# Two fp32 layers behind attention on one core: another order of the seven products, other banks, other homes

## The chip, the cores and the metric

The kernel runs on one core of one Trainium2 chip. The metric is the device time of one execution in microseconds; a kernel's time is the median of its runs. A core has TensorE (matmuls into the eight banks of PSUM), VectorE, ScalarE and GpSimd for element work, and SyncE, whose queue issues the DMAs here. Each engine works through its own instructions in a fixed order; a semaphore holds an instruction until what it needs is done, and everything behind it on that engine waits too.

## What is computed

Attention with a window of 128 over 4 x 8 heads of 576 positions, then two feed-forward layers on the 2304 x 512 tokens that come out, all in fp32:

```python
attn_out = _attn_ref(q, k, v)                      # window 128, slopes per head, softmax
x = attn_out.transpose(0, 2, 1, 3).reshape(2304, 512)
g = x @ w_gate; val = x @ w_val                    # layer one, 512 -> 1536
x = (g * sigmoid(g) * val) @ w_out                 # 1536 -> 512
h = x @ w_in                                       # layer two, 512 -> 2048
y = (h * tanh(softplus(h))) @ w_out                # 2048 -> 512
```

## The kernel before

**fp32 as three products.** TensorE multiplies in a rounded format (F32R). Every fp32 operand is split into a high part (rounded on ScalarE, `hi_act`, line 124) and a low part (the rest, on VectorE, `lo_dve`, line 127), and each product is three matmuls: high x high, high x low, low x high. All are issued at line 117. A tile that is split is therefore ready only when both engines have had it.

**Layer one** runs over five chunks of tokens (512, 384, 512, 512, 384). For each of 12 slices of the 1536 there is a pair of groups `g`, `v` (`gv_groups`: the hidden values into `g_ps`, then two VectorE steps at lines 603 and 611, then the split into `hh` and `hl`) and a group `o` that multiplies `hh`, `hl` by the output weights into four accumulators `acc0` to `acc3`. `o` runs some slices behind `g`, `v`: that distance is the lag, `CFG["lastlag"]` in the last chunk. At the end `evacuate` copies the accumulators out, two by ScalarE (line 580) and two by VectorE (line 581), as `ev`.

**Layer two** uses a scheme of the Winograd kind: a 2 x 2 block product with seven products rather than eight, of sums of blocks. It runs in three passes `p` over two blocks of TB = 384 tokens each.

- *First product* (`hidden`, for each of eight `j`): TensorE multiplies `win` (the weights' sums, split) by `xs1` to `xs7` (the tokens' sums, split) in the order 1, 6, 7, 5, 2, 4, 3, six matmuls each; product 2 adds onto the bank of 1, and 3 onto the bank of 5, so a `j` needs five banks. VectorE's `add` (line 666) and ScalarE join them to the hidden values `G`. The tokens' sums `xr` are made by VectorE (line 666).
- *The weights' sums* (`make_win`): four subtractions on GpSimd (line 754) into a tile `t4`, then the split into `win`, ScalarE and VectorE in two steps each, one from the raw weights `w4` and one from `t4`. There is one buffer for `t4`: GpSimd starts on the next when both engines have read it.
- *Second product*: for each product `i` of ORDER2, and each of four `q`, `operands` gives one split tile `op` of sums of `G` (five buffers), which TensorE multiplies by `wout` for m = 0 and m = 1, six matmuls each. So `i` takes 48 matmuls and two banks, a pass 336. `outputs` joins the products to `v` and `y` on VectorE (line 666), and ScalarE copies product 2 (line 860). Product 4 stays in its bank until 7 is done; then `done(2, ...)` subtracts it (`y<-v,bk`), which frees the bank.
- *Loads and stores*: `wout` comes in halves of 1 MB (line 763, three buffers), a pass 14 of them; a finished block of 768 tokens goes out as `yT` (line 865). Both stand in SyncE's queue.

**Banks.** `bank` (lines 654 to 659) hands out two kinds in turn: one of four that rotate, and one of four that are fixed by name, `acc0` to `acc3`, in a ring. A bank is written again when its last reader is done.

**Homes.** Tiles of layer two lie where layer one's tiles lay before them, on the weight tiles `wt` of the last chunk and others; each waits until the last reader of what it lies on is done. Which `wt` that is follows from the order in which the tiles of the pool `br` are asked for; `wt` of slice i is free when group i of the last chunk is done.

**Order.** TensorE's order is that of the program text. For the other engines a planner sets the order by its own idea of the times when the program is built; it is fixed then.

Of the kernel before, what the change touches and what calls it, by code (L numbers as in the profile page):

```python
# [29 lines left out]

SLOT = {1: 0, 2: 1, 3: 2, 5: 3, 6: 4, 7: 5, 4: 6}
CFG = dict(
    order="SSOTT", delay0=2, early=[4], pbufs=10, pump_g=2, pump_p=2, lag=4, lastlag=4, evprio=500,
    conv_a=0.1, conv_b=0.9,
)

# [60 lines left out]
def body(ctx: ExitStack, tc: tile.TileContext, qT, kT, vP, w1, w1o, w2, cst, yT):  # L97
# [495 lines left out]
    def gv_groups(ci, i):  # L593
        p = plansA[ci]
        n = p.n
        st = {}

        def g():
            need(("w", i))
            st["g"] = hid(x_t[ci], n, wt[i], 0)  # L600
            t = hp_.tile([128, 512], F32, tag="t", name="t")
            tanhs.append(nc.scalar.activation(out=t[:, :n], in_=st["g"][:, :n], func=AF.Tanh, scale=0.5))  # L602
            nc.vector.scalar_tensor_tensor(  # L603
                out=t[:, :n], in0=t[:, :n], scalar=1.0, in1=st["g"][:, :n], op0=ALU.add, op1=ALU.mult
            )
            st["t"] = t

        def v():
            vps = hid(x_t[ci], n, wt[i], 512)
            t = st["t"]  # L610
            nc.vector.scalar_tensor_tensor(  # L611
                out=t[:, :n], in0=t[:, :n], scalar=0.5, in1=vps[:, :n], op0=ALU.mult, op1=ALU.mult
            )
            if ci == len(plansA) - 1:
                hh = bpool["p"].tile([128, 512], F32R, tag="hhb", name="hh", bufs=CFG["lag"])
                hl = bpool["p"].tile([128, 512], F32R, tag="hlb", name="hl", bufs=CFG["lag"])
            else:
                hh = hp_.tile([128, 512], F32R, tag="hh", name="hh", bufs=2)
                hl = hp_.tile([128, 512], F32R, tag="hl", name="hl", bufs=2)
            hi_act(hh[:, :n], t[:, :n])  # L620
            lo_dve(hl[:, :n], t[:, :n], hh[:, :n])
            hs["A", ci, i] = (hh, hl)

        return [g, v]
# [29 lines left out]
    def bank():  # L654
        banks[0] += 1
        c, odd = divmod(banks[0], 2)
        if odd:
            return rot("bk")
        return ps.tile([128, 512], F32, tag=f"acc{c % CT}", name="bk", bufs=1)
# [24 lines left out]
            )  # L684
        return r

    def x_parts(bp, r):
        xs = {i: bp.tile([128, 2, 2, TB], F32R, tag=f"xs{i}", name=f"xs{i}", bufs=1) for i in range(1, 8)}
# [12 lines left out]
        part(xs[5], a22)  # L701
        part(xs[3], a12)
        return xs

    def products(bk, ws, xs, first, last):

# [4 lines left out]
            mm(o, wh, xl, False, False)  # L711
            mm(o, wl, xh, False, last and c == n - 1)

    def outputs(i, bk, u, new, done):


        bk = bk[:, :TB]
        if i == 1:
            u["c"] = new()
            nc.scalar.activation(out=u["c"], in_=bk, func=AF.Copy)  # L720
        elif i == 6:
            u["a"] = u.pop("c")
            add(u["a"], u["a"], bk)
        elif i == 7:
            u["b"] = new()
            add(u["b"], u["a"], bk)
        elif i == 5:
            done(3, u["b"], bk)
        elif i == 2:
            done(0, bk, None)  # L730
        elif i == 3:
            done(1, u["a"], bk)
        else:
            done(2, u["b"], bk)

    def layer2(br):
        G = {}
        win, wout = {}, {}
        ORDER1 = (1, 6, 7, 5, 2, 4, 3)
        ORDER2 = (4, 1, 6, 7, 5, 2, 3)  # L740
        onto = {2: 1, 3: 5}

        raws = {}

        def load_raw(p, j):
            raws[p, j] = br.tile([128, 4, 256], F32, tag="w4", name="w4", bufs=2)
            nc.sync.dma_start(out=raws[p, j], in_=w2d[j].rearrange("p (k n) -> p k n", k=4))

        def make_win(p, j):

            w = raws.pop((p, j))
            x = br.tile([128, 4, 256], F32, tag="t4", name="t4", bufs=1)
            for o, a, b in ((0, w[:, 0], w[:, 1]), (1, w[:, 3], x[:, 0]), (2, w[:, 3], w[:, 0]), (3, x[:, 1], w[:, 2])):
                nc.gpsimd.tensor_tensor(out=x[:, o], in0=a, in1=b, op=ALU.subtract)  # L754
            t = win[p, j] = br.tile([128, 2, 7, 256], F32R, tag="win", name="win")
            for d, src in ((slice(0, 3), w[:, 1:4]), (slice(3, 7), x)):
                hi_act(t[:, 0, d], src)
                lo_dve(t[:, 1, d], src, t[:, 0, d])
# [6 lines left out]
        def hidden(p, j, xs):  # L765
            w = win.pop((p, j))
            q, jj = divmod(j, 2)
            if jj == 0:
                G[p, q] = bp.tile([128, 4, 2, TB], F32, tag=f"g{q}", name="G", bufs=1)
            g = G[p, q]  # L770
            u = {}

            def new():
                return bp.tile([128, TB], F32, tag="u", name="u", bufs=6)

            def done(k, a, b):
                if b is None:
                    mish(g[:, k, jj], a)
                    return
                add(g[:, k, jj], a, b, ALU.subtract if k == 2 else ALU.add)  # L780
                mish(g[:, k, jj], g[:, k, jj])

            bks = {}
            for i in ORDER1:
                bk = bks[i] = bks[onto[i]] if i in onto else bank()
                s = SLOT[i]
                products(
                    bk, [(w[:, 0, s, c:c + 128], w[:, 1, s, c:c + 128]) for c in (0, 128)],
                    [(xs[i][:, 0, c], xs[i][:, 1, c]) for c in range(2)], i not in onto, i not in onto.values(),
                )  # L790
                outputs(i, bk, u, new, done)

        def operands(p, i):

# [12 lines left out]
                    add(g[:, 2], g[:, 1], g[:, 0], ALU.subtract)  # L807

        load_raw(0, 0)
        xr = load_x(br, 0)  # L810
        load_raw(0, 1)
        xs = x_parts(br, xr)
        for j in range(2):
            make_win(0, j)
            load_raw(0, j + 2)
# [2 lines left out]
        for p in range(NPB):  # L818
# [16 lines left out]
            left = [[2, 2], [2, 2]]  # L835
            t0 = 2 * p * TB
            for i in ORDER2:
                bks = held[i] = held[onto[i]] if i in onto else [bank(), bank()]
                for q, o in enumerate(operands(p, i)):
                    k, jq = divmod(2 * q, NJ // 2)  # L840
                    if (p, i, k) not in wout:
                        load_wout(p, i, k)
                        loads.remove((i, k))
                    w = wout[p, i, k]
                    if jq == 0 and loads:
                        load_wout(p, *loads.pop(0))
                    for m in range(2):
                        products(
                            bks[m],
                            [(w[:, jq + e, 0, 128 * m:128 * m + 128], w[:, jq + e, 1, 128 * m:128 * m + 128]) for e in range(2)],  # L850
                            [(o[:, 0, e], o[:, 1, e]) for e in range(2)],
                            i not in onto and q == 0, i not in onto.values() and q == NJ // 2 - 1,
                        )
                for m in range(2):

                    def done(k, a, b, m=m):
                        t, f = divmod(k, 2)
                        y = ys[f][m]
                        if b is None:
                            nc.scalar.activation(out=y[:, t], in_=a, func=AF.Copy)  # L860
                        else:
                            add(y[:, t], a, b, ALU.subtract if k == 2 else ALU.add)
                        left[f][m] -= 1
                        if not left[f][m]:
                            nc.sync.dma_start(out=yr[:, 2 * f + m, t0:t0 + 2 * TB], in_=y.rearrange("p a t -> p (a t)"))
# [7 lines left out]
                    outputs(i, bks[m], us[m], new, done)  # L873
                    if i == 7:
                        done(2, us[m]["b"], us[m]["p4"])
                if p + 1 < NPB:
                    if i == 7:
                        xs = x_parts(br, xr)
                    if i in (5, 2):
                        j = (5, 2).index(i)  # L880
                        make_win(p + 1, j)
                        load_raw(p + 1, j + 2)

# [164 lines left out]
```

## Time and profile before

| what | us |
|---|---|
| median of 3 runs | 1038.94 |
| lowest and highest of them | 1038.35, 1039.30 |
| profiled execution, its own time | 1040.23 |
| span of its profile | 1038.4 |

The profiled execution is 1.29 us above the median. TensorE is the busiest engine; its time by kind of work is in part 5 of the page, its pauses in the table of waits, and where they lie in its timeline. The first pass of layer two begins near 640 us in the trace; the second products of the three passes begin at 712, 844 and 974 us. A "releaser" is what ended the pause before a piece. PEclk is the granted clock as a share of 2.4 GHz.

### The profile page before, as it was taken

The page shows a single profiled execution, that of the slowest core. Times are in us where ns is not written, and L with a number is a line of the kernel's source. Part 1 is how long each engine was busy: PE and PEld are TensorE (multiplying, and loading weights), DVE is VectorE, ACT ScalarE, POOL GpSimd, SP SyncE. Part 2 cuts the span into 40 slices and gives each one's busy share as a digit, 9 for nine tenths or more (in the row PEclk, how much of TensorE's full clock was granted, in tenths as well). Part 3 has the DMA queues.
Part 4 walks back from the last instruction along what each step waited for, and adds up shares of the span by engine and source line. Part 5 has one row for each costly group of instructions (what it writes and reads, how often), then busy time and mean ns, then how long its engine had stood idle before and what let it go on. Part 6 is the DMA issues. An engine that isn't in the chain of part 4 may idle for free.

```text
span 1038.4 us, 14510 instructions
## 1 busy us (share of the span) xinstructions
PE 985.0 (95%) x5168; PEld 863.1 (83%) x5168; DVE 701.0 (68%) x1241; ACT 550.9 (53%) x1121; POOL 180.1 (17%) x204
## 2 busy tenths in 40 slices
PE   6899999999999999999999997899889998799998
PEld 4566777898987777788888997899889998799998
DVE  4988887777667644468534577778845788557763
ACT  6867564757666654455443445456423565235442
POOL 2610000000000000000002444433701438013000
PEclk7989999999999999999999999899989999899999
DMA  8854423486355631246404996425655156560275
GB/s 301 271 200 138 157 79 124 136 254 185 90 175 166 213 85 48 99 150 234 133 1 138 338 348 226 175 72 176 222 181 200 62 175 230 181 201 24 76 249 182
DMA packets 74935, 173.89 MB, mean 167 GB/s; under 512 B 8432, under 2 KB 50032, under 8 KB 65136
## 3 DMA queue, kind: packets, MB, share of 16 engines
q1 hardware_dynamic: 74864, 172.98, 50.1%
q8 instruction: 40, 0.66, 0.3%
q14 instruction: 31, 0.25, 0.1%
HBM read 137.30 MB, written 35.65 MB: 167 GB/s over the span
## 4 chain that ended last, share of the span: by engine, by line
PE 76%; DVE 9%; POOL 5%; DMA 5%; ACT 2%; issue 1%; SPq 1%; DVEq 0%; POOLq 0%; ACTq 0%
PE g_ps L117 28%; PE bk L117 23%; PE acc L117 13%; PE o_ps L117 5%; POOL t L754 5%; PE s_ps L117 4%; PE t_ps L259 3%; DVE G L666 2%; DVE op L127 2%; DVE win L127 2%; DMA w2d<-cw 1%; POOL Pt L249 1%; DMA wst<-w 1%; DVE xs L127 1%; DMA wraw<-w1o 1%
## 5 line engine op out<-in xcount | busy, mean ns | idle before, releaser
L117 PE MATMUL g_ps<-xt,w 128*128 128x512 f32 (+1 forms) x1440 | 322.0, 375 | 0.3 <-ACT PT L271 0.3
L117 PEld LDWEIGHTS g_ps<-xt,w 128*128 128x128 f32 x1440 | 259.5, 188 | 40.3 <-issue 3.3
L117 PE MATMUL bk<-op,wout 128*128 128x384 f32 x1008 | 183.5, 342 | 19.5 <-DVE y L666 12.7
L117 PEld LDWEIGHTS bk<-op,wout 128*128 128x128 f32 x1008 | 179.5, 193 | 23.0 <-DVE y L666 13.7
L117 PE MATMUL bk<-xs,win 128*128 128x384 f32 x1008 | 179.9, 338 | 11.8 <-ACT xs L124 6.9
L117 PEld LDWEIGHTS bk<-xs,win 128*128 128x128 f32 x1008 | 176.9, 190 | 14.4 <-ACT xs L124 7.3
L117 PE MATMUL acc<-hh,ring 128*128 128x512 f32 (+1 forms) x480 | 149.6, 374 | 0.0
L754 POOL TENSOR_TENSOR t<-w 128x256 f32<-128x256 f32 x48 | 82.9, 1747 | 209.7 <-DVE win L127 198.1
L124 ACT ACTIVATE op<-G 128x768 fp32r<-128x768 f32 x84 | 69.1, 842 | 69.9 <-PE bk L117 66.6
L127 DVE TENSOR_TENSOR op<-G,op 128x768 fp32r<-128x768 f32 x84 | 80.9, 973 | 35.9 <-ACT op L124 35.8
L117 PEld LDWEIGHTS acc<-hh,ring 128*128 128x128 f32 x480 | 89.1, 188 | 13.8 <-issue 1.9
L117 PE MATMUL acc<-hl,ring 128*128 128x512 f32 (+1 forms) x240 | 88.4, 368 | 0.0
L230 ACT ACTIVATE Pt<-Pt,sm 128x256 f32<-128x256 f32 (+2 forms) x160 | 74.6, 468 | 17.4 <-DVE sm L226 16.9
L226 DVE CUSTOM_DVE_ANT_0 Pt<-s_ps,cst_sb 128x256 f32<-128x256 f32 (+2 forms) x160 | 54.4, 376 | 35.4 <-PE s_ps L117 35.2
L602 ACT ACTIVATE t<-g_ps 128x512 f32<-128x512 f32 (+1 forms) x60 | 33.0, 550 | 77.4 <-PE g_ps L117 77.2
L603 DVE SCALAR_TENSOR_TENSOR t<-t,g_ps 128x512 f32<-128x512 f32 (+1 forms) x60 | 37.7, 628 | 52.3 <-ACT t L602 52.2
L611 DVE SCALAR_TENSOR_TENSOR t<-t,g_ps 128x512 f32<-128x512 f32 (+1 forms) x60 | 37.9, 632 | 41.8 <-PE g_ps L117 40.7
L666 DVE TENSOR_TENSOR G<-u,bk 128x384 f32<-128x384 f32 x72 | 39.3, 552 | 36.5 <-PE bk L117 34.4
L209 POOL MEMSET sm<- 128x8 f32 x40 | 4.9, 134 | 339.4 <-ACT Pt L247 311.2
L993 ACT ACTIVATE G<-G 128x384 f32<-128x384 f32 x72 | 37.0, 518 | 49.8 <-DVE G L666 49.8
L124 ACT ACTIVATE hh<-t 128x512 fp32r<-128x512 f32 (+1 forms) x60 | 34.9, 582 | 52.8 <-DVE t L611 46.9
L541 POOL TENSOR_TENSOR cw<-cw 128x256 f32<-128x256 f32 x32 | 28.9, 926 | 192.8 <-DMA cw<-w2d 192.3
(71 smaller groups left out, 1304.9 us busy)
## 6 DMA issues: line engine op xcount, KB each, us to landing
wout<-w2o SPq DMA_DIRECT2D x42, 1024.0 KB, 5.2
wraw<-w SPq DMA_DIRECT2D x16, 1024.0 KB, 5.4
w2o<-chl SPq DMA_DIRECT2D x16, 896.0 KB, 6.0
wst<-w SPq DMA_DIRECT2D x12, 1024.0 KB, 8.2
cw<-w1od SPq DMA_DIRECT2D x24, 512.0 KB, 4.3
w<-w2d SPq DMA_DIRECT2D x24, 512.0 KB, 3.4
w2d<-cw SPq DMA_DIRECT2D x16, 512.0 KB, 3.7
wraw<-w1o SPq DMA_DIRECT2D x6, 1024.0 KB, 6.2
```

The source lines that it names most:

```text
L117: nc.tensor.matmul(out=out, lhsT=lhsT, rhs=rhs, start=start, stop=stop, skip_group_check=True)
L124: nc.scalar.activation(out=out, in_=in_, func=AF.Copy)
L127: nc.vector.tensor_tensor(out=out, in0=in_, in1=hi.bitcast(F32), op=ALU.subtract)
L226: nc.vector.tensor_tensor_reduce(out=Pt[:q.qn, :w], in0=s_ps[:q.qn, q.so:q.so + w], in1=nb[:q.qn, 128 - q.kn:128 + q.qn], op0=ALU.add, op1 ...
L230: nc.scalar.activation(out=Pt[:q.qn, :w], in_=Pt[:q.qn, :w], func=AF.Exp, scale=-1.0, bias=sm[:q.qn, i:i + 1], accum_out=sm[:q.qn, 8 + i:9 ...
L259: nc.tensor.transpose(t_ps[:x.n, o:o + q.qn], Pt[:q.qn, c0:c0 + x.n], ident[:q.qn, :q.qn])
L602: tanhs.append(nc.scalar.activation(out=t[:, :n], in_=st["g"][:, :n], func=AF.Tanh, scale=0.5))
L603: nc.vector.scalar_tensor_tensor(out=t[:, :n], in0=t[:, :n], scalar=1.0, in1=st["g"][:, :n], op0=ALU.add, op1=ALU.mult)
L611: nc.vector.scalar_tensor_tensor(out=t[:, :n], in0=t[:, :n], scalar=0.5, in1=vps[:, :n], op0=ALU.mult, op1=ALU.mult)
L666: nc.vector.tensor_tensor(out=out, in0=a, in1=b, op=op)
L754: nc.gpsimd.tensor_tensor(out=x[:, o], in0=a, in1=b, op=ALU.subtract)
L993: nc.scalar.activation(out=out, in_=in_, func=AF.Mish)
```

## The change

ORDER2 is changed from 4, 1, 6, 7, 5, 2, 3 to 4, 1, 6, 7, 2, 5, 3. In the second product only 2 still adds onto another's banks (1's); 3 gets two of its own, and for that VectorE adds product 5 to `u["a"]`, two additions a pass. The next pass's weights' sums hang on products 2 and 5, in that order. In the last chunk of layer one the lag is 3 rather than 4, and `hh` and `hl` have five buffers rather than four. `t4` is one tile, asked for once, and the first tiles of layer two are asked for in another order (`x_tiles` is split from `x_parts`).

```diff
-    ... lag=4, lastlag=4, evprio=500,
+    ... lag=4, lastlag=3, evprio=500,
...
-                hh = bpool["p"].tile([128, 512], F32R, tag="hhb", name="hh", bufs=CFG["lag"])
+                hh = bpool["p"].tile([128, 512], F32R, tag="hhb", name="hh", bufs=CFG["lastlag"] + 2)
...
+    def x_tiles(bp, which):
+        return {i: bp.tile([128, 2, 2, TB], F32R, tag=f"xs{i}", name=f"xs{i}", bufs=1) for i in which}
...
         elif i == 5:
+            if not joined:
+                add(u["a"], u["a"], bk)
             done(3, u["b"], bk)
...
-        ORDER2 = (4, 1, 6, 7, 5, 2, 3)
+        ORDER2 = (4, 1, 6, 7, 2, 5, 3)
         onto = {2: 1, 3: 5}
+        onto2 = {2: 1}
...
-            x = br.tile([128, 4, 256], F32, tag="t4", name="t4", bufs=1)
+            x = t4
...
         load_raw(0, 0)
+        t4 = br.tile([128, 4, 256], F32, tag="t4", name="t4", bufs=1)
+        xs = x_tiles(br, (7, 5))
         xr = load_x(br, 0)
+        xs.update(x_tiles(br, (1, 4, 6, 2, 3)))
         load_raw(0, 1)
-        xs = x_parts(br, xr)
+        x_parts(xs, xr)
...
-                bks = held[i] = held[onto[i]] if i in onto else [bank(), bank()]
+                bks = held[i] = held[onto2[i]] if i in onto2 else [bank(), bank()]
...
-                    if i in (5, 2):
-                        j = (5, 2).index(i)
+                    if i in (2, 5):
+                        j = (2, 5).index(i)
```

The homes that come of it: `t4` lay over `wt` 11, now over `wt` 6; the first `xr` over `wt` 6 and 10, now 0 and 1; the first `win` over 0, 8 and 9, now 3, 5 and 8; `xs7` over 4 and 11, now 6 and 10.

VectorE, first pass, second product, before. The names: `op` is an operand tile, `G` the next operand's sum, `v` a running sum of products, `y` the output; `y_6682` and `y_6683` take product 4 off for m = 0 and 1. The first four `op` rows are product 5's, the last is product 2's.

```order
L666 TENSOR_TENSOR v_6828<-v_6828,bk_6831 128x384
L127 TENSOR_TENSOR op_7005<-G_6137,op_7005 128x768
L666 TENSOR_TENSOR G_6421<-G_6421 128x768
L666 TENSOR_TENSOR G_6554<-G_6554 128x768
L127 TENSOR_TENSOR op_7022<-G_6280,op_7022 128x768
L127 TENSOR_TENSOR op_7037<-G_6421,op_7037 128x768
L127 TENSOR_TENSOR op_7054<-G_6554,op_7054 128x768
L666 TENSOR_TENSOR v_6972<-v_6826,bk_6902 128x384
L666 TENSOR_TENSOR v_6975<-v_6828,bk_6903 128x384
L127 TENSOR_TENSOR op_7083<-G_6137,op_7083 128x768
L666 TENSOR_TENSOR y_6682<-v_6972,bk_6686 128x384
L666 TENSOR_TENSOR y_6683<-v_6975,bk_6687 128x384
```

The same place now. The first four `op` are product 2's, those from `op_7077` on product 5's; `y_6675` and `y_6676` take product 4 off.

```order
L127 TENSOR_TENSOR op_6996<-G_6135,op_6996 128x768
L666 TENSOR_TENSOR G_6415<-G_6415 128x768
L127 TENSOR_TENSOR op_7013<-G_6276,op_7013 128x768
L666 TENSOR_TENSOR G_6547<-G_6547 128x768
L127 TENSOR_TENSOR op_7028<-G_6415,op_7028 128x768
L127 TENSOR_TENSOR op_7045<-G_6547,op_7045 128x768
L666 TENSOR_TENSOR v_6965<-v_6819,bk_6895 128x384
L666 TENSOR_TENSOR v_6968<-v_6821,bk_6896 128x384
L127 TENSOR_TENSOR op_7077<-G_6135,op_7077 128x768
L666 TENSOR_TENSOR y_6675<-v_6965,bk_6679 128x384
L127 TENSOR_TENSOR op_7094<-G_6276,op_7094 128x768
L666 TENSOR_TENSOR y_6676<-v_6968,bk_6680 128x384
```

Product 2's operands now come where product 5's were, and the two `y` stand with `op` tiles of product 5 around them rather than behind product 2's first.

VectorE, start of layer two, before, from the first two `xs` on. `win<-t4` is the second part of the weights' split, `ev` the copy of an accumulator of layer one.

```order
L127 TENSOR_TENSOR xs1_6013<-xr_6008,xs1_6013 128x768
L127 TENSOR_TENSOR xs2_6014<-xr_6008,xs2_6014 128x768
L127 TENSOR_TENSOR win_6043<-t4_6038,win_6043 128x1024
L127 TENSOR_TENSOR xs4_6016<-xr_6008,xs4_6016 128x768
L581 COPY ev_6110<-acc1_5593 128x384
L666 TENSOR_TENSOR xr_6008<-xr_6008 128x768
L127 TENSOR_TENSOR win_6055<-w4_6011,win_6055 128x768
L581 COPY ev_6114<-acc3_5595 128x384
```

The same place now.

```order
L127 TENSOR_TENSOR xs1_6026<-xr_6023,xs1_6026 128x768
L127 TENSOR_TENSOR xs2_6029<-xr_6023,xs2_6029 128x768
L581 COPY ev_6109<-acc1_5549 128x384
L127 TENSOR_TENSOR win_6055<-t4_6020,win_6055 128x1024
L581 COPY ev_6113<-acc3_5551 128x384
L127 TENSOR_TENSOR xs4_6027<-xr_6023,xs4_6027 128x768
L127 TENSOR_TENSOR win_6066<-w4_6031,win_6066 128x768
L666 TENSOR_TENSOR xr_6023<-xr_6023 128x768 x3
```

`ev` of the second accumulator now stands ahead of the first `win<-t4`, `xs4` behind it, and the sums `xr` behind both `ev`.

SyncE's queue, first pass, second product, before: loads of `wout`, and the stores `yT`.

```order
L763 DMA wout<-w2o 128x2048 x6
L865 DMA yT<-y 128x768
L763 DMA wout<-w2o 128x2048
L865 DMA yT<-y 128x768
L763 DMA wout<-w2o 128x2048
L865 DMA yT<-y 128x768
L763 DMA wout<-w2o 128x2048
```

The same place now.

```order
L767 DMA wout<-w2o 128x2048 x4
L872 DMA yT<-y 128x768
L767 DMA wout<-w2o 128x2048
L872 DMA yT<-y 128x768
L767 DMA wout<-w2o 128x2048 x3
L872 DMA yT<-y 128x768
L767 DMA wout<-w2o 128x2048
```

The first two stores now stand ahead of the two loads for product 3, which were among the six loads in front of them.

## Rows read from the trace of the kernel before

**Rows 1.** Page, part 1: engine, busy us, share of the span, instructions.
```profile
PE 985.0 (95%) x5168; PEld 863.1 (83%) x5168; DVE 701.0 (68%) x1241; ACT 550.9 (53%) x1121; POOL 180.1 (17%) x204
```

**Rows 2.** Waits of TensorE: us in total, times, longest.
```profile
PE bk L117 <- DVE y L666: 12.7, 3, 5.8
...
PE bk L117 <- DVE op L127: 6.6, 5, 2.0
```

**Rows 3.** Timeline, TensorE, first pass: start, us, work, count, idle before and releaser.
```profile
747.34 5.31 PE L117 MATMUL bk<-op,wout 128*128 128x384 f32 x29 [1.25 <-DVE op L127]
758.04 26.26 PE L117 MATMUL bk<-op,wout 128*128 128x384 f32 x138 [5.39 <-DVE y L666]
```

**Rows 4.** Timeline, TensorE, second pass.
```profile
879.97 3.22 PE L117 MATMUL bk<-op,wout 128*128 128x384 f32 x17 [0.46 <-DVE op L127]
889.00 25.65 PE L117 MATMUL bk<-op,wout 128*128 128x384 f32 x138 [5.81 <-DVE y L666]
```

**Rows 5.** Timeline, TensorE, third pass.
```profile
1010.11 24.20 PE L117 MATMUL bk<-op,wout 128*128 128x384 f32 x138 [1.53 <-DVE y L666]
```

**Rows 6.** Timeline, VectorE, first pass, second product.
```profile
743.78 1.23 DVE L127 TENSOR_TENSOR win<-t,win 128x1024 fp32r<-128x1024 f32 x1 [3.91 <-ACT win L124]
...
745.79 2.90 DVE L127 TENSOR_TENSOR op<-G,op 128x768 fp32r<-128x768 f32 x2
...
755.19 1.00 DVE L666 TENSOR_TENSOR v<-v,bk 128x384 f32<-128x384 f32 x2
756.11 0.94 DVE L127 TENSOR_TENSOR op<-G,op 128x768 fp32r<-128x768 f32 x1
756.98 1.00 DVE L666 TENSOR_TENSOR y<-v,bk 128x384 f32<-128x384 f32 x2
```

**Rows 7.** Timeline, GpSimd, layer two.
```profile
630.23 1.43 POOL L754 TENSOR_TENSOR t<-w 128x256 f32<-128x256 f32 x2 [11.64 <-PE g_ps L117]
...
638.82 2.79 POOL L754 TENSOR_TENSOR t<-w 128x256 f32<-128x256 f32 x2 [5.65 <-DVE win L127]
...
720.84 20.32 POOL L754 TENSOR_TENSOR t<-w 128x256 f32<-128x256 f32 x2 [8.63 <-DVE win L127]
```

**Rows 8.** Windows: us, busy of PE, PEld, DVE, ACT, POOL; PEclk, DMA, GB/s.
```profile
756.00:760.00 4.00, 1.96 (x6) 1.96 (x7) 1.99 (x4) 0.00 (x0) 0.00 (x0) 0.50 0.01 2
888.00:892.00 4.00, 3.00 (x9) 3.01 (x10) 0.94 (x3) 0.68 (x1) 0.00 (x0) 0.50 0.00 0
1008.00:1012.00 4.00, 2.47 (x15) 2.15 (x14) 2.06 (x4) 0.96 (x2) 0.00 (x0) 1.00 0.84 264
```

**Rows 9.** Timeline, TensorE, start of layer two.
```profile
640.39 1.22 PE L117 MATMUL bk<-xs,win 128*128 128x384 f32 x6
648.56 0.69 PE L117 MATMUL bk<-xs,win 128*128 128x384 f32 x1 [6.95 <-ACT xs L124]
651.88 22.06 PE L117 MATMUL bk<-xs,win 128*128 128x384 f32 x113 [2.63 <-DVE xs L127]
```

**Rows 10.** Timeline, VectorE, start of layer two.
```profile
637.52 1.22 DVE L127 TENSOR_TENSOR win<-t,win 128x1024 fp32r<-128x1024 f32 x1
638.66 0.95 DVE L127 TENSOR_TENSOR xs<-xr,xs 128x768 fp32r<-128x768 f32 x1
639.54 0.56 DVE L581 COPY ev<-acc 128x384 f32<-128x384 f32 x1
640.02 1.00 DVE L666 TENSOR_TENSOR xr<-xr 128x768 f32<-128x768 f32 x1
...
643.75 1.47 DVE L127 TENSOR_TENSOR xs<-xr,xs 128x768 fp32r<-128x768 f32 x1
```

**Rows 11.** Windows: the last chunk of layer one (columns of Rows 8).
```profile
569.00:640.00 71.00, 71.00 (x407) 71.00 (x406) 44.30 (x53) 31.38 (x42) 26.30 (x29) 1.00 0.94 321
```

**Rows 12.** Page, part 6: DMA issues, count, KB each, us to landing.
```profile
wout<-w2o SPq DMA_DIRECT2D x42, 1024.0 KB, 5.2
```

**Rows 13.** Page, part 5: busy us, mean ns, then idle before.
```profile
L666 DVE TENSOR_TENSOR G<-u,bk 128x384 f32<-128x384 f32 x72 | 39.3, 552 | 36.5 <-PE bk L117 34.4
```

More of the change, by code (lines that the diff above doesn't have):

```diff
@@ L32 @@
 CFG = dict(
-    order="SSOTT", delay0=2, early=[4], pbufs=10, pump_g=2, pump_p=2, lag=4, lastlag=4, evprio=500,
+    order="SSOTT", delay0=2, early=[4], pbufs=10, pump_g=2, pump_p=2, lag=4, lastlag=3, evprio=500,
     conv_a=0.1, conv_b=0.9,
@@ L614, in v @@
             if ci == len(plansA) - 1:
-                hh = bpool["p"].tile([128, 512], F32R, tag="hhb", name="hh", bufs=CFG["lag"])
-                hl = bpool["p"].tile([128, 512], F32R, tag="hlb", name="hl", bufs=CFG["lag"])
+                hh = bpool["p"].tile([128, 512], F32R, tag="hhb", name="hh", bufs=CFG["lastlag"] + 2)
+                hl = bpool["p"].tile([128, 512], F32R, tag="hlb", name="hl", bufs=CFG["lastlag"] + 2)
             else:
@@ L685, in load_x, with x_parts @@
         return r
-    def x_parts(bp, r):
-        xs = {i: bp.tile([128, 2, 2, TB], F32R, tag=f"xs{i}", name=f"xs{i}", bufs=1) for i in range(1, 8)}
+    def x_tiles(bp, which):
+        return {i: bp.tile([128, 2, 2, TB], F32R, tag=f"xs{i}", name=f"xs{i}", bufs=1) for i in which}
+    def x_parts(xs, r):
         a11, a12, a21, a22 = r[:, 0, 0], r[:, 0, 1], r[:, 1, 0], r[:, 1, 1]
@@ L702, in x_parts @@
         part(xs[3], a12)
-        return xs
     def products(bk, ws, xs, first, last):
@@ L712, in products, with outputs @@
             mm(o, wl, xh, False, last and c == n - 1)
-    def outputs(i, bk, u, new, done):
+    def outputs(i, bk, u, new, done, joined):
         bk = bk[:, :TB]
@@ L790, in hidden @@
                 )
-                outputs(i, bk, u, new, done)
+                outputs(i, bk, u, new, done, True)
         def operands(p, i):
@@ L851, in layer2 @@
                             [(o[:, 0, e], o[:, 1, e]) for e in range(2)],
-                            i not in onto and q == 0, i not in onto.values() and q == NJ // 2 - 1,
+                            i not in onto2 and q == 0, i not in onto2.values() and q == NJ // 2 - 1,
                         )
@@ L872, in layer2 @@
                         continue
-                    outputs(i, bks[m], us[m], new, done)
+                    outputs(i, bks[m], us[m], new, done, False)
                     if i == 7:
@@ L877, in layer2 @@
                     if i == 7:
-                        xs = x_parts(br, xr)
-                    if i in (5, 2):
-                        j = (5, 2).index(i)
+                        xs = x_tiles(br, range(1, 8))
+                        x_parts(xs, xr)
+                    if i in (2, 5):
+                        j = (2, 5).index(i)
                         make_win(p + 1, j)
```

## The prediction

> **What bounds the kernel now.** Read the page's busy row first: TensorE is busy 985.0 of 1038.4 us [rows 1]. Every product is made of the same number of matmuls before and after, so only TensorE's pauses, and the matmuls that run at a lower clock behind a pause, can be won or lost; VectorE, ScalarE and the queues count only where TensorE waits for them. Next the table of TensorE's waits: the largest entry is VectorE's `y` subtraction, three waits and 12.7 us, 5.8 at most; `op` tiles cost 6.6 us in five [rows 2]. The timeline of TensorE shows where the three lie: one in each pass over 768 tokens, 5.39, 5.81 and 1.53 us, always with 138 matmuls left in the pass [rows 3 to 5]. A pass has 336 here, 48 for each product: with 138 left, products 4, 1, 6 and 7 (192) are done, and of product 5 the six of m = 0, so what waits is product 5's m = 1. Its bank is one of the fixed four and was product 4's; it comes free when VectorE has subtracted product 4 from the output (`y<-v,bk`). VectorE's queue shows why that is late: `win<-t` at 743.78 waited 3.91 us, and the `op`, `G`, `v` and `y` behind it run without a gap until 757.98; TensorE goes on at 758.04 [rows 3, 6].
>
> The stretches of the clock tell the rest: 0.50 around each of the first two waits (the lower level, 1.2 of 2.4 GHz), 1.00 at the third [rows 8]. TensorE stood still for over 5 us before the clock fell, for 1.53 us where it stayed. The same 138 matmuls took 26.26 and 25.65 us behind the long waits, 24.20 behind the short one [rows 3 to 5]: the clock costs 2.06 and 1.45 us more.
>
> **The change part by part.** The 1.29 us between the profiled execution (1040.23) and the median (1038.94) is taken as an offset: the sum is made in the trace and set against the median.
>
> *Order 4,1,6,7,2,5,3.* Product 2 follows 7 and adds onto product 1's banks, which are open: it needs no bank and so no `y`. Product 5's m = 1 still needs product 4's bank, but 48 matmuls later, and at full clock 138 take 24.20 us, 0.175 each, so 8.4 us later [rows 5]. Is VectorE done by then? In the first pass TensorE has 29 matmuls from 747.34 in 5.31 us, the last six of product 5, so product 7 ends at about 751.6 [rows 3]; product 2 then ends at 760.0 and product 5 asks for the bank at 761.0. VectorE's row ends its `win<-t` at 745.0 and has, in the new order, eight `op`, three `G`, four `v` and two `y` to go. At the row's own prices (`op` 1.45 for the first two beside GpSimd, 0.95 after, `G` 0.95, `v` and `y` 0.50) that is 8.6 + 2.9 + 3.0 = 14.5 us at most, done by 759.5 [rows 6]: 1.5 us ahead. Product 2's first `op` is done by the same prices at 750.8, 0.8 us before product 7 ends, and the next at 752.7, 1.0 before its turn. In the second pass the same reckoning starts from product 7's end at 882.1 (17 matmuls from 879.97, six of them of product 5 [rows 4]) and leaves about as much. So the waits go, and with them the low clock: 5.39 + 2.06 = 7.45 in the first pass, 5.81 + 1.45 = 7.26 in the second, 1.53 in the last; **-16.2 us**. `op` ahead of `G` at the first rows in the new queue could give back up to 0.7 of TensorE's wait of 1.25 there [rows 3]; I take none of it and keep it for the range.
>
> *Banks for product 3.* 12 banks a pass rather than 10, out of the same eight. Product 3's m = 1 gets product 1's fixed bank, freed by a ScalarE copy behind product 2, one product (8.4 us) before it is needed: nothing. Product 3 is no longer summed onto 5 in PSUM, so VectorE adds 5 to `u` itself: six more additions. No such row exists; the nearest is the same operation on the same shape, 0.552 us [rows 13], 3.3 us in all, beside product 3's 8.4 us of matmuls in each pass. Uncovered, it would be 1.1 us a pass; covered, nothing. I take nothing, since VectorE then has only product 3's four `op` and two `y` besides.
>
> *Lag three, five buffers.* In the last chunk of layer one TensorE is busy 71.00 of 71.00 us [rows 11]: no wait to take away, and a group of 24 matmuls changes places with one of 12. Nothing is gained; a loss would need `hh` to be later than three groups, which I bound at 0.5 us. I take zero.
>
> *Homes.* This moves the start of layer two. GpSimd's first `t` stands idle 11.64 us for a matmul group of layer one; its tile now lies over a weight tile that is free earlier. But this `t` took 1.43 us from 630.23 [rows 7] and does not end the chain: product 6 waits for the last `xs`, 6.95 us for ScalarE's part and 2.63 for VectorE's, until 651.88 [rows 9]. Ahead of it on VectorE stands the second `win<-t`, which waits for GpSimd's second group, released by VectorE's first `win<-t` (ends 638.74; GpSimd starts at 638.82 [rows 7, 10]). In the new VectorE order the eviction `ev` comes ahead of that `win<-t`, and `ev` needs the second accumulator's last matmul, which is six matmuls of 0.175 us before layer one ends at 640.4 [rows 9], so about 639.4: it starts at 639.54 [rows 10] and can hardly start sooner. So the first `win<-t` ends at 639.54 + 0.5 + 1.2, about 641.2, and GpSimd's second group starts 2.4 us later than now. From there: four GpSimd steps as at 638.82 (5.6 us, to 646.9), ScalarE's and VectorE's `win<-t` (1.1 and 1.2, to 649.2), then `xs5`, `xr`, `xs7`, `xs6`. With GpSimd's third group beside them these take 1.47 or so each, as `xs` at 643.75 did, alone 0.95 as at 638.66 [rows 10]. TensorE goes on at 654.9 with the first price, 653.0 with the second; if GpSimd's steps too are as fast as its first ones (2.9 us for four), 650.8. I choose **+2.7 us**, near the first, since before, too, GpSimd's third group ran beside the last `xs`. The bounds are -1.1 (650.8) and +3.8: the latter if GpSimd gets no step in beside VectorE's run from 641.8 to 647.3 and does its last three only then.
>
> That upper bound has a row: two `t` steps from 720.84 took 20.32 us while VectorE ran without a pause, where two from 630.23 took 1.43 [rows 7]. The Trainium skill, on the page "SBUF — State Buffer", section "Who interferes with whom", says that a VectorE instruction with two SBUF inputs and a GpSimd instruction that reads SBUF exclude each other for the length of an instruction. The trace agrees with its 20.32 us. By that rule alone `ev`, which reads PSUM, would not be in GpSimd's way but `xs`, `win` and `xr` would, and the term would be +3.8, the time 1.1 us longer. It speaks against what the homes are for, and leaves the order of products alone.
>
> **Sum.** -16.2 + 2.7 = -13.5, so 1038.94 - 13.5 = **1025.4 us** (a profiled execution of about 1026.7).
>
> **The rivals.**
> (a) *The start of layer two gains.* All bounds low: -16.2 - 0.7 - 1.1 = -18.0, 1020.9. For it: GpSimd's 11.64 us of idleness goes. Against: the place of `ev` in VectorE's queue. 10%.
> (b) *The `op` tiles become the wait.* The pause at `y` also gave VectorE time to catch up. Without it product 2's `op` are due 2.1 us apart right behind product 7; if GpSimd's `t` beside them makes each `op`, `G` and `v` half as slow again, as the first two `op` were (1.45 each [rows 6]), VectorE's 14.5 us become some 19, and TensorE waits about 3 us in each of the first two passes, for `op` or, at product 5, for the same `y`. With the low clock's part, half of 14.7 us is lost: 1032.8. For it: five waits for `op` stand in the table already [rows 2]. Against: GpSimd's group behind 743.78 is short. 18%, the wait's return at product 5 among it.
> (c) *The change does not do it:* the wait moves to product 3's banks in full. It would need ScalarE's copy behind product 2 to be over 8 us late; no row shows that. Within 0.2% of before. 2%.
> (d) *Slower: weights late behind outputs.* In SyncE's queue the loads of `wout` for product 3 now stand behind two `yT` that wait for product 2's outputs. Such a load takes 5.2 us to land [rows 12], and has product 5's 8.4 us. It is bounded by the 3.2 us of slack: if `yT` is issued more than that late, TensorE waits at product 3. Beyond 6 us of delay a pass the pauses, with 2 us of clock each, cost (6 - 3.2 + 2) x 3 = 14.4 us and eat the gain of 13.5; at 9 us late they cost 23.4 and the time is 1048.8. Against: the table of TensorE's waits has no load of `wout` in layer two. 4%.
>
> **How the numbers follow.** The forecast has 66%. The range goes from rival (a), 1020.5, to just below rival (b)'s full size, 1032.0; it leaves out (c), (d), and part of (b), some 15%. A difference of 0.2%, 2.1 us, is about what a measurement of this kernel tells from none. Faster by more: the forecast, (a) and nearly all of (b), 92%; the same 3%; slower 5%.
>
> **What would show it.** Right: no wait for `y` at product 5 in any pass, 1.00 of the clock there, some 7.4, 7.3 and 1.5 us less from each pass's first second-product matmul to its last; product 6 of the first j at 653 to 655 rather than 651.88; VectorE's first `win<-t` behind `ev`. Wrong: a wait of 2 us or more for `op` inside product 2, for `y` at product 5, for a load at product 3, or a start of layer two before 651.

## The result

The changed kernel takes 1024.87 us (median of 4 runs, 1022.81 to 1025.72) against 1039.12 for the kernel before in the same set: a ratio of 0.986, 95% interval 0.9843 to 0.9877, so 12.8 to 16.3 us faster. The forecast was 1025.4 us.

The profiled execution took 1022.81 us, 2.06 below its median, where that of before was 1.29 above its own. This matters for the comparison: layer two begins at 637.02 in the trace of after and at 640.39 in that of before, 3.37 us apart, which is about 1.29 + 2.06. The profiles of the experiments below reach it between 636.3 and 638.3 us, with old and new parts alike, the attention and layer one coming first. So 3.37 of the 17.4 us between the two spans (1038.4 and 1021.0) belong to the runs, and 14.0 to the change.

The page's busy row of after (engine, busy us, share, instructions) and its waits of TensorE (total, times, longest):

```profile
PE 982.3 (96%) x5168; PEld 861.5 (84%) x5168; DVE 704.1 (69%) x1247; ACT 550.5 (54%) x1121; POOL 183.2 (18%) x204
```

```profile
PE bk L117 <- DVE op L127: 4.9, 4, 2.0
...
PE bk L117 <- DMA wout<-w2o: 1.5, 2, 1.0
```

The `y` row of [rows 2], 12.7 us, is gone. `op` fell from 6.6 to 4.9; `xs`, at the start of layer two, rose from 6.95 + 2.63 [rows 9] to 7.95 + 4.03 (shown below); loads of `wout` are new, 1.5 us in two. The timeline of TensorE shows the second products of the three passes (start, us, work, count, the pause before with its releaser):

```profile
732.37 14.47 PE L117 MATMUL bk<-op,wout 128*128 128x384 f32 x72 [1.99 <-DVE op L127]
747.30 27.14 PE L117 MATMUL bk<-op,wout 128*128 128x384 f32 x155 [0.46 <-DVE op L127]
...
870.12 18.84 PE L117 MATMUL bk<-op,wout 128*128 128x384 f32 x107 [0.47 <-DVE op L127]
889.95 8.56 PE L117 MATMUL bk<-op,wout 128*128 128x384 f32 x48 [0.98 <-DMA wout<-w2o]
...
957.94 50.11 PE L117 MATMUL bk<-op,wout 128*128 128x384 f32 x288
1008.57 8.59 PE L117 MATMUL bk<-op,wout 128*128 128x384 f32 x48 [0.51 <-DMA wout<-w2o]
```

No piece waits for `y`. In the first pass 155 matmuls run from 747.30 to the end, over the place where 138 waited 5.39 us [rows 3]; in the third 288 run in one piece. The clock stays up there. The windows of after answer to two of [rows 8] (busy of PE, PEld, DVE, ACT, POOL, then PEclk):

```profile
756.00:760.00 4.00, 4.00 (x25) 4.00 (x24) 3.78 (x5) 2.41 (x5) 0.00 (x0) 1.00 0.98 320
888.00:892.00 4.00, 3.02 (x18) 2.73 (x17) 2.62 (x5) 0.00 (x0) 0.00 (x0) 1.00 0.95 344
```

At the start of layer two the timeline of TensorE, answering to [rows 9], reads:

```profile
637.02 1.22 PE L117 MATMUL bk<-xs,win 128*128 128x384 f32 x6
646.20 0.69 PE L117 MATMUL bk<-xs,win 128*128 128x384 f32 x1 [7.95 <-ACT xs L124]
650.92 21.52 PE L117 MATMUL bk<-xs,win 128*128 128x384 f32 x113 [4.03 <-DVE xs L127]
```

By stages, from one start on TensorE to the next, in the two profiled executions:

| stage | before | after | difference | forecast |
|---|---|---|---|---|
| up to layer two | 640.39 | 637.02 | -3.37 | 0 |
| start of layer two (product 1 to the last wait for `xs`) | 11.49 | 13.90 | +2.41 | +2.7 |
| rest of the first pass's first products | 60.61 | 60.10 | -0.51 | 0 |
| second products, first pass | 71.65 | 63.26 | -8.39 | -7.45 |
| second pass | 70.79 | 64.50 | -6.29 | -7.26 |
| third pass | 60.24 | 59.22 | -1.02 | -1.53 |
| behind the last matmul | 4.09 | 3.84 | -0.25 | 0 |

The first products of the second and third pass take 59.6 us in both. The second products together give 15.7 us where 16.2 were forecast.

### The profile page after: what moved, and what is told of

It is laid out like the page before. It is cut to its first block, busy times and chain, and to the rows that moved or that the text cites. A ratio compares the mean times of both kernels' runs of the same rounds, so it can differ in the third digit from the quotient of the medians.

```text
span 1021.0 us, 14513 instructions
## 1 busy us (share of the span) xinstructions
PE 982.3 (96%) x5168; PEld 861.5 (84%) x5168; DVE 704.1 (69%) x1247; ACT 550.5 (54%) x1121; POOL 183.2 (18%) x204
## 4 chain that ended last, share of the span: by engine, by line
PE 77%; DVE 8%; DMA 5%; POOL 5%; ACT 2%; issue 2%; SPq 1%; DVEq 0%; ACTq 0%; POOLq 0%
PE g_ps L117 28%; PE bk L117 24%; PE acc L117 14%; PE o_ps L117 5%; POOL t L758 4%; PE s_ps L117 4%; PE t_ps L259 3%; DMA wout<-w2o 2%; DVE G L666 1%; DVE win L127 1%; DMA wraw<-w 1%; DVE op L127 1%; POOL Pt L249 1%; DVE xs L127 1%; DVE xr L666 1%
## 5 line engine op out<-in xcount | busy, mean ns | idle before, releaser
L117 PE MATMUL bk<-op,wout 128*128 128x384 f32 x1008 | 180.9, 340 | 6.4 <-DVE op L127 4.9
L230 ACT ACTIVATE Pt<-Pt,sm 128x256 f32<-128x256 f32 (+2 forms) x160 | 74.6, 467 | 16.7 <-DVE sm L226 16.3
```

The lines of the kernel that those rows point to most:

```text
L117: nc.tensor.matmul(out=out, lhsT=lhsT, rhs=rhs, start=start, stop=stop, skip_group_check=True)
L230: nc.scalar.activation(out=Pt[:q.qn, :w], in_=Pt[:q.qn, :w], func=AF.Exp, scale=-1.0, bias=sm[:q.qn, i:i + 1], accum_out=sm[:q.qn, 8 + i:9 ...
```

## The experiments

Each time is the median of the kernel's runs with the ratio to the kernel before in the same set; sets differ by up to 1.5 us in the time of the kernel before, so times of different sets are compared by their ratios, and parts of a kernel by their traces.

**e1: the new order alone.** Lag, buffers and homes go back.

```diff
-    ... lastlag=3, ...          hh, hl: bufs=CFG["lastlag"] + 2
+    ... lastlag=4, ...          hh, hl: bufs=CFG["lag"]
-        t4 = br.tile(...)
-        xs = x_tiles(br, (7, 5))
         xr = load_x(br, 0)
-        xs.update(x_tiles(br, (1, 4, 6, 2, 3)))
+        xs = x_tiles(br, range(1, 8))      # behind load_raw(0, 1); t4 in make_win
```

> The new order and product 3's own banks alone; lag, buffers and homes as before. What is read is the start of layer two, from product 1's first matmul to the matmuls behind the last wait for xs: 11.49 us before, 13.90 after the change. Both theories (the lag moved ev, or the homes did) expect 11.5 here, as before. Second products as after the change: about 8.4, 6.3 and 1.0 us shorter than before. Time: about 2.4 us below the changed kernel's 1024.9, so 1022.5.

1021.65 us, ratio 0.9842 (0.9827 to 0.9857). TensorE's timeline: the start of layer two, the first pass's second products, the third pass's product 3.

```profile
636.61 1.22 PE L117 MATMUL bk<-xs,win 128*128 128x384 f32 x6
...
648.11 21.99 PE L117 MATMUL bk<-xs,win 128*128 128x384 f32 x113 [2.64 <-DVE xs L127]
...
743.55 29.23 PE L117 MATMUL bk<-op,wout 128*128 128x384 f32 x167 [1.25 <-DVE op L127]
...
1006.42 8.59 PE L117 MATMUL bk<-op,wout 128*128 128x384 f32 x48 [1.10 <-DMA wout<-w2o]
```

The start takes 648.11 - 636.61 = 11.50 us, as before. By the trace the second products are 7.73, 7.50 and 0.44 us shorter than before, 15.7 us in all, as in the changed kernel. So the order wins its part alone; lag and homes together bring the 2.4 us at the start.

**e2: without the lag.** Lag four and four buffers, as in e1's first lines; homes as changed.

> The change with its lag and buffers undone (lag four, four buffers), homes as changed. Theory one, the lag: ev stands behind the first win<-t4 in VectorE's queue again, the start of layer two takes 11.5 us or a little less (GpSimd's first subtractions come earlier but end no chain), and the time is some 2.4 us below the changed kernel's, about 1022.5. Theory two, as the prediction had it, the homes: the start stays at 13.9 and the time at 1024.9.

1022.52 us, ratio 0.9853 (0.9832 to 0.9873). TensorE's timeline at the start of layer two:

```profile
637.22 1.23 PE L117 MATMUL bk<-xs,win 128*128 128x384 f32 x6
...
648.72 22.28 PE L117 MATMUL bk<-xs,win 128*128 128x384 f32 x113 [2.63 <-DVE xs L127]
```

11.50 us: with the new homes and the old lag the start is what it was.

**e3: without the homes.** Lag three and five buffers as changed; `t4` and `xs` as in e1's last lines.

> The change with its homes undone, lag three and five buffers kept. Theory one, the lag: ev stays ahead of the first win<-t4, the start stays at 13.9 us or above (GpSimd's first subtractions now wait for the last group of layer one), time 1024.9 or up to 2 us more. Theory two, the homes: the start falls to 11.5 and the time to about 1022.5.

1023.78 us, ratio 0.9863 (0.9848 to 0.9878). The same places of TensorE's timeline:

```profile
637.87 1.23 PE L117 MATMUL bk<-xs,win 128*128 128x384 f32 x6
...
651.77 21.65 PE L117 MATMUL bk<-xs,win 128*128 128x384 f32 x113 [4.03 <-DVE xs L127]
...
748.25 18.82 PE L117 MATMUL bk<-op,wout 128*128 128x384 f32 x107 [0.47 <-DVE op L127]
```

13.90 us with the old homes. So the lag lengthens the start, and the homes do nothing to it either way. The lag and the five buffers were only changed together; which of the two does it is not shown. The chain that sets it is seen in VectorE's row of after:

```profile
636.18 0.56 DVE L581 COPY ev<-acc 128x384 f32<-128x384 f32 x1 [2.62 <-PE acc L117]
636.65 1.22 DVE L127 TENSOR_TENSOR win<-t,win 128x1024 fp32r<-128x1024 f32 x1
...
640.81 3.86 DVE L666 TENSOR_TENSOR xr<-xr 128x768 f32<-128x768 f32 x3
644.59 1.22 DVE L127 TENSOR_TENSOR win<-t,win 128x1024 fp32r<-128x1024 f32 x1
...
647.99 4.27 DVE L127 TENSOR_TENSOR xs<-xr,xs 128x768 fp32r<-128x768 f32 x3
```

`ev` comes first and waits 2.62 us for layer one's accumulator, the first `win<-t` stands behind it, and product 6's `xs` is the second of the last three. GpSimd's first subtractions start 9.43 us before layer two, where they started 10.16 before it [rows 7, 9]: the new home of `t4` does not make them earlier. Its second ones follow `win<-t` as they did:

```profile
627.59 1.44 POOL L758 TENSOR_TENSOR t<-w 128x256 f32<-128x256 f32 x2 [11.04 <-DMA w<-w2d]
...
637.95 2.12 POOL L758 TENSOR_TENSOR t<-w 128x256 f32<-128x256 f32 x2 [7.40 <-DVE win L127]
```

In VectorE's order `ev` stands ahead of `win<-t` in the kernels with lag three, and behind it in e1 and e2. Why the planner turns the two round was not tried. With lag three the last `g_ps` group of layer one starts 12.6 us before layer two rather than 14.6, so what follows it on VectorE is later too; that this is the reason is a guess. The lag gives something back: the third piece of e1 waits 1.25 us for `op`, as before the change [rows 3], that of e3 0.47, since another order of `op` and `G` goes with it.

**e4: lag, buffers and homes alone.** The second product goes back to the old order and banks.

```diff
-        ORDER2 = (4, 1, 6, 7, 2, 5, 3)
+        ORDER2 = (4, 1, 6, 7, 5, 2, 3)
-        onto2 = {2: 1}
+        onto2 = {2: 1, 3: 5}                # and no addition of 5 to u["a"]
```

> Lag, buffers and homes as changed; the order of the second product and its banks as before. Both theories: the waits for y come back at product 5 (5.4, 5.8 and 1.5 us), the low clock behind the first two of them too, and the start of layer two takes 13.9 us: 2.4 us above the kernel before, so about 1041.4 against 1039. If the homes and the lag gain elsewhere, it is 1039 or less.

1041.03 us, ratio 1.0028 (1.0019 to 1.0038): slower than before. TensorE's timeline, the pieces with 138 matmuls left:

```profile
757.23 26.20 PE L117 MATMUL bk<-op,wout 128*128 128x384 f32 x138 [5.78 <-DVE y L666]
...
888.41 25.54 PE L117 MATMUL bk<-op,wout 128*128 128x384 f32 x138 [5.06 <-DVE y L666]
...
1009.42 24.20 PE L117 MATMUL bk<-op,wout 128*128 128x384 f32 x138 [1.53 <-DVE y L666]
```

The waits for `y` are back at product 5. The order is worth some 16 us by itself (e1), the rest costs 2 to 4.

**e5: product 3 onto 5's banks.**

```diff
-        onto2 = {2: 1}
+        onto2 = {2: 1, 3: 5}                # and no addition of 5 to u["a"]
```

> The change with one part undone: product 3 is summed onto product 5's banks again, so VectorE has two additions fewer a pass. Theory one, the own banks are part of the gain: 3 now follows 5 at once and its first matmul must wait until VectorE has read 5's bank for m = 0. That read can start when 5's last six matmuls for m = 1 begin, 1.04 us ahead, and takes 0.55: a wait for y of 0.3 to 2 us at product 3 in each pass, 1 to 6 us in all, 1026 to 1031. Theory two, the order alone does it: no wait there, and the time of the change, 1024.9.

1024.89 us, ratio 0.9876 (0.9859 to 0.9894). TensorE's waits:

```profile
PE bk L117 <- DVE y L666: 1.1, 2, 0.7
...
PE bk L117 <- DMA wout<-w2o: 0.7, 1, 0.7
```

The wait that theory one names is there, 0.39 us in the first pass and 0.72 in the third, but at its smallest; in the second pass the load of `wout` is what comes last. Against the 1.5 us of waits for loads in the changed kernel that is 0.3 us more; the interval overlaps the change's own. By the trace the second products of the three passes are 0.7 us longer in all. The own banks of product 3 are worth no time that these runs resolve.

**e6: own banks, old order.** ORDER2 as in e4, `onto2` as changed.

> The change with the order 4,1,6,7,5,2,3 as before, product 3's own banks kept. The theory (product 5's m = 1 waits for product 4's bank, and what lies between 7 and 5 hides it): the waits for y come back at product 5, 5 to 6 us in the first two passes and 1.5 in the last, with the low clock behind the first two, 1041. The rival (too few banks in all is what makes TensorE wait, whatever the order): the waits shrink and the time comes under 1035.

1040.01 us, ratio 1.002 (1.0011 to 1.003). TensorE's waits:

```profile
PE bk L117 <- DVE y L666: 12.4, 3, 5.8
```

All three waits are there. It is the order that takes them away, not the number of banks.

**e7: the stores behind the loads.** On e1; a `yT` is issued only when the newest load of `wout` has been.

```diff
-                            nc.sync.dma_start(out=yr[...], in_=y...)
+                            stores.append((2 * f + m, y))
...
+            def flush():        # behind the next product's loads, and at the end
+                for k, y in stores:
+                    d = nc.sync.dma_start(out=yr[:, k, ...], in_=y...)
+                    tc.add_manual_dep(d.ins, newest[0].ins.name, behind, ...)
```

> The new order and own banks alone, lag, buffers and homes as before, and the two stores yT behind product 2 held back in SyncE's queue until both loads of wout for product 3 are issued. Theory one (the loads for product 3 land late, 9.3 us instead of 5.4, since the stores go ahead of them): the wait for wout at product 3 (0.5 to 1.1 us) goes and that load lands in 5 to 7 us; second products of the last pass 59.2 to 58.7 us; time 0.5 to 1.5 us below that of the order alone, 1021.65. Theory two (it lands late for another reason): the wait stays.

1020.24 us, ratio 0.9834 (0.9815 to 0.9854); e1's was 0.9842, so the time alone does not tell them apart. The trace does. In the changed kernel SyncE's queue in the second pass reads:

```profile
880.16 0.34 SPq L872 DMA_DIRECT2D yT<-y  x1
880.67 0.32 SPq L767 DMA_DIRECT2D wout<-w2o  x1
881.20 1.04 SPq L872 DMA_DIRECT2D yT<-y  x1
```

The load for product 3's first half is issued at 880.67 between two stores and lands 9.1 us later, where the median load takes 5.4; TensorE waits for it until 889.95. With the stores behind both loads (e7) it lands after 5.1 us in the first two passes and 5.8 in the third, and no wait for `wout` is left in any pass; the third is one piece:

```profile
955.75 58.43 PE L117 MATMUL bk<-op,wout 128*128 128x384 f32 x336
```

That is theory one. But two stores around a load do not suffice to make it late: in the first pass of the changed kernel the same load, issued at 757.83 between stores at 757.31 and 758.35, landed after 5.9 us, and in e1 it took 5.8, 6.3 and 9.3 us in the three passes. What makes the difference was not tried.

**e8: the sums later.** On e7; the next pass's `xr` and `xs`, but for `xs1` and `xs4`, are ordered behind product 2's first operand on VectorE and ScalarE.

```diff
-                    if i == 7:
-                        x_parts(xs, xr)
+                    if i == 2:
+                        x_parts(xs, xr, made[2, 0])
...
+    def gated(ins, e):          # called for each step of part and add
+        if gate[e] is not None:
+            tc.add_manual_dep(ins.ins, gate[e].ins.name, held_behind, ...)
```

> As e7, and most of the next pass's sums xr and xs are held back in the planner until product 2's first operand is made, so that VectorE has only op, G and win to make while products 4 to 7 run. The theory (VectorE's queue between products 4 and 7 is what makes the waits for op left there, 2.0 and 0.5 to 1.25 us in each of the first two passes, and what starves GpSimd's subtractions for 20 us): the waits for op go, about 5.6 us with little of the low clock, and the stretch of 20 us on GpSimd shortens to a few: 1021 - 5.6 = 1015. The rival (the sums are then late for the next pass, or y at product 5 is late): waits for xs at the start of the next pass or for y at product 5 come in and eat 2 us or more of it.

1009.70 us, ratio 0.9728 (0.9713 to 0.9744), 5 us better than the theory asked. TensorE's second products are one piece each:

```profile
710.02 58.66 PE L117 MATMUL bk<-op,wout 128*128 128x384 f32 x336
...
828.11 58.43 PE L117 MATMUL bk<-op,wout 128*128 128x384 f32 x336
...
945.97 58.43 PE L117 MATMUL bk<-op,wout 128*128 128x384 f32 x336
```

No wait for `op` is left, nor for `y` or a load. From their start to the next stage's, the second products of the first two passes took 63.95 and 63.28 us in e7, 58.50 and 58.27 in e8: 10.5 us, of which e7's waits for `op` there are 1.97 + 1.24 + 1.98 + 0.47 = 5.7. The expectation counted these alone. Most of the rest is the clock: in e7 it goes down behind the waits of 1.97 and 1.98 us, as the windows of e7 show (columns as above). The 60 matmuls behind the first took 12.26 us where 60 at full clock take 10.5, the 72 behind the second 14.46 where 72 take 12.6: 3.6 of the 4.8 us. From e7, the waits for `op` in all, the two pieces and the windows:

```profile
PE bk L117 <- DVE op L127: 5.7, 4, 2.0
...
730.61 12.26 PE L117 MATMUL bk<-op,wout 128*128 128x384 f32 x60 [1.97 <-DVE op L127]
...
854.23 14.46 PE L117 MATMUL bk<-op,wout 128*128 128x384 f32 x72 [1.98 <-DVE op L127]
...
730.00:734.00 4.00, 3.39 (x14) 3.40 (x15) 4.00 (x6) 2.07 (x3) 4.00 (x1) 0.73 0.12 49
854.00:858.00 4.00, 3.77 (x13) 3.77 (x14) 4.00 (x6) 1.69 (x3) 4.00 (x1) 0.59 0.08 27
```

GpSimd's stretch shortens, but to half only:

```profile
717.20 10.62 POOL L770 TENSOR_TENSOR t<-w 128x256 f32<-128x256 f32 x2 [7.46 <-DVE win L127]
```

**e9: the old order, sums later.** The gate of e8 and the stores of e7 on the kernel before; the sums stand behind product 5's first operand and product 4's `y`.

```diff
+                    if i == 5:
+                        x_parts(xs, xr, (made[5, 0][0], made["y"]))
```

> The kernel before in its order 4,1,6,7,5,2,3 and with 3 summed onto 5, lag and homes as before, but with the next pass's sums xr and xs held back until product 5's first operand and product 4's subtraction y are made. Question: how much of the old waits for y (5.4, 5.8, 1.5 us) was the order of the products, and how much VectorE's queue of sums ahead of it? Theory one, mostly the queue: the waits for op go and those for y shrink to the last pass's 1.5 us in every pass (there no sums ran), the clock stays at 1.00, a pass's second products take about 60.0 us, and the time is 3 x 1.5 us above e8's 1009.7, about 1014. Theory two, mostly the order: the waits for y stay at 4 us or more with the low clock behind them, 1024 or more.

1014.04 us, ratio 0.9777 (0.9755 to 0.9798). TensorE's pieces behind product 5's first six matmuls:

```profile
744.77 24.19 PE L117 MATMUL bk<-op,wout 128*128 128x384 f32 x138 [1.53 <-DVE y L674]
...
864.44 24.19 PE L117 MATMUL bk<-op,wout 128*128 128x384 f32 x138 [1.53 <-DVE y L674]
...
984.11 24.19 PE L117 MATMUL bk<-op,wout 128*128 128x384 f32 x138 [1.53 <-DVE y L674]
```

Three times 1.53 us, at full clock, and no wait for `op`. This is theory one to the hundredth: of the old 5.39 and 5.81 us the order of the products had made 1.53, and what stood in VectorE's queue ahead of `y` the rest, with the low clock.

That was not the sums alone. The kernel before had the second `win<-t` ahead of `y` too, and VectorE stood 3.91 us for it [rows 6], because GpSimd's steps for it had taken 20.32 us beside VectorE's unbroken run [rows 7]. In e9 the planner put this split behind `y` together with the sums; the second `y` starts at 744.17, and VectorE's row goes on:

```profile
759.46 1.23 DVE L127 TENSOR_TENSOR win<-t,win 128x1024 fp32r<-128x1024 f32 x1
```

How much of the rest was the sums' own time and how much the wait for `win` was not taken apart.

**e10: the start.** On e8; the sums for product 6 go ahead of the second split of weights.

```diff
+            part(xs[2], a12)
+            six = part(xs[6], a11)
+            if behind[0] is None:
+                gate[:] = six
...
             make_win(0, j)
+            gate[:] = made_x        # xs5: the second win behind it
```

> As e8, and at the start of layer two the sums for product 6 go ahead of the second weights' split in VectorE's and ScalarE's queues. Theory (the start is set by what stands in VectorE's queue ahead of product 6's xs, win and its GpSimd step above all, as the prediction's chain has it): the start of layer two falls from 11.5 us to 4.5 to 6.5, and the time by 5 to 7 us to about 1003.5, if no later xs or win is late instead. The rival: the second win is then late for the second j and TensorE waits for it there, 3 us or more.

1005.87 us, ratio 0.9688 (0.9668 to 0.9708), the fastest of all: 32.8 us below the kernel before in its set and, by the ratios, some 18 below the change. TensorE's timeline at the start of layer two, and its waits for `G`:

```profile
637.70 1.22 PE L117 MATMUL bk<-xs,win 128*128 128x384 f32 x6
...
643.05 22.51 PE L117 MATMUL bk<-xs,win 128*128 128x384 f32 x113 [0.30 <-DVE xs L127]
```

```profile
PE bk L117 <- DVE G L674: 4.0, 6, 1.3
```

The start takes 5.35 us, as the theory has it, 6.1 less than in e8. The time fell by less, by some 4 us by the ratios where 5 to 7 were expected, since some is given back: the waits for `G`, 2.2 us in six in e8, are 4.0, and the first products behind the start take 62.84 us where e8's took 60.78.

## Why the prediction was right, and where its steps were not

**The bound and the waits.** TensorE's three waits for `y` were read rightly, and so was what ends them: product 4's bank. They went when 2 was put between 7 and 5, and came back when that alone was undone (e6; in e4 together with the banks). The margin held too: product 5 was to ask for the bank about 1.5 us behind VectorE's `y`. In after, product 7 ends about 749.2 (11 of 155 matmuls from 747.30), product 2 at 757.6, so product 5's m = 1 is due at 758.6; VectorE's row:

```profile
755.26 0.54 DVE L666 TENSOR_TENSOR y<-v,bk 128x384 f32<-128x384 f32 x1
755.73 0.94 DVE L127 TENSOR_TENSOR op<-G,op 128x768 fp32r<-128x768 f32 x1
756.60 0.54 DVE L666 TENSOR_TENSOR y<-v,bk 128x384 f32<-128x384 f32 x1
```

ends the second `y` at 757.14, 1.5 us ahead.

One reading of the clock was wrong: TensorE had not stood still for over 5 us before it fell. It stopped at 752.65 and the clock was already 0.50 in the window from 756.00 [rows 3, 8]. It also fell behind a wait for `op` of 1.98 us, to 0.50 from 736 to 738 before and from 734 to 736 after. The sum did not suffer, since the change leaves that wait as it was.

**The size of the waits.** 16.2 us were forecast for the second products and 15.7 came. First pass: 8.39 where 7.45 was said; 0.8 of the 0.9 more are the `op` wait of 1.25 that became 0.46, the term of 0.7 that was left out and kept for the range. It came with the lag, not with the order (e1 against e3). Second pass: 6.29 where 7.26 was said, third 1.02 where 1.53 was: rival (d), small. Its working took 5.2 us for a load of `wout`, the median of the row, and so 3.2 us of slack; between two stores the load landed 9.1 and 8.7 us after its issue, where TensorE came for it after 8.3, and TensorE waited 0.98 and 0.51 us. The bound that failed is the median as a landing time for a load that has a store on both sides. Rival (b) did not come: the waits for `op` fell from 6.6 to 4.9 us. The clock's share was right in sign and place: 1.00 where it was 0.50.

That the total, 1025.4 against 1024.87, is so close is in part luck: 0.9 us more in the first pass and 1.5 less in the other two nearly cancel. The offset of 1.29 us did not carry over: the profiled execution was to take about 1026.7 and took 1022.81.

**The start.** +2.7 us was forecast and +2.41 measured, by the chain that was named: `ev` ahead of the first `win<-t`, GpSimd's second group behind that, then the sums. But the working put it under the homes, and took nothing for the lag. That is wrong: the homes alone leave it at 11.50 (e2), the lag alone brings 13.90 (e3). The new order of the queue was read off the changed kernel as a whole, where three edits stand together, and was put down to the one that moved tiles. The rival from the Trainium skill, that GpSimd is held out by VectorE's instructions with two inputs in SBUF ("SBUF — State Buffer", section "Who interferes with whom"), gave 1.1 us more for this term. It did not come: GpSimd's two steps at 637.95 took 2.12 us beside VectorE, and its four were done at 642.9. VectorE's three `xr` took 3.86 us, 1.29 each, where one takes 0.95 alone (before, at 646.67). That both engines grew slower agrees with the rule, instruction by instruction; what failed is the extension that VectorE's run would keep GpSimd out to its end. Why it did so at 720.84 [rows 7] and not here is not shown.

**The cause behind the cause.** The prediction saw VectorE run without a gap up to `y`, and took the order of products for the whole cure. e9 shows that the order had 1.53 us a pass in it. The other 3.86 and 4.28, the low clock and the waits for `op` came from work for the next pass that stood in VectorE's queue between products 4 and 7: the sums, and the split `win<-t` that they had made late. The change hides the late `y` under product 2. Taking the sums out of the way in the old order (e9) gives 1038.69 - 1014.04 = 24.65 us, more than the change, and both together more still (e8). For the forecast this made no difference; for what to do next it does.

**The added work.** The six additions on VectorE show nowhere, as said. That product 3's banks would cost nothing was right, and e5 shows that they also gain nothing to speak of.

## What to carry to other kernels

When an engine waits for a step of another, read what stands in that engine's queue ahead of the step before changing what needs it: work that is due a stage later can go behind it, and that took away here most of a wait that the reordering only covered. An edit to a lag or a buffer count can move instructions of other stages where a planner sets the order; build each part of a change alone, and compare the queues, before a cost is put down to one of them. The median landing time of a kind of transfer is no bound for one of them: with stores on both sides a load took up to 1.7 times as long.

## What the hardware showed beyond that

- A load of 1 MB that lands in 5.4 us at the median took 5.9, 9.1 and 8.7 us between two stores of 384 KB in the same queue, in the three passes of the changed kernel, and 5.1 to 5.8 with both stores behind it (e7). Why the first pass differs is open.
- The clock fell in pauses of 5.39 and 5.81 us, and behind 1.97 and 1.98 in e7 too, and stayed at 1.00 behind 1.53 us (the third pass before, [rows 5, 8]). In e7 a pause of two microseconds for `op` so cost nearly twice its length.
- Two subtractions on GpSimd took 20.32 us beside an unbroken run of VectorE [rows 7] and 10.62 beside a shorter one (e8); both times they ended just behind it, at 741.16 where the run ended at 739.87, and at 727.82 where it ended at 727.23. Two at 630.23, with VectorE nearly idle, took 1.43. TensorE waited for nothing of it in e8.
